# Attention into experts: zeroes at item eight, the first unit rounded at item seventeen, GpSimd's squares in halves, VectorE's order in the tail

## The chip, the core and the metric

The kernel runs on one core of a Trainium2 chip. The metric is the time of one execution on the device, in microseconds. Five engines take part: TensorE (PE, with its weight load PEld), VectorE (DVE), ScalarE (ACT), GpSimd (POOL) and SyncE (SP), which issues most of the DMAs. Each engine runs its own instructions in the order in which they stand, and waits on semaphores for the others.

## What is computed

An attention with random features, then eight experts with one expert per token, then a feed-forward layer with softplus. The inputs are float32: q, k and v of 4 x 8 x 576 x 64, 128 features; 2304 tokens of 512; experts of 512 x 1024 x 512; a last layer of 512 x 2048 x 512.

```python
def phi(x):                                   # x is q or k, scaled
    proj = np.einsum('bhsd,md->bhsm', x, omega)
    h = proj - np.sum(x * x, axis=-1, keepdims=True) / 2.0
    h = h - np.max(h, axis=-1, keepdims=True)
    return np.exp(h) / np.sqrt(m)
kv  = np.einsum('bhsm,bhsd->bhmd', k_p, v);  z = np.sum(k_p, axis=2)
num = np.einsum('bhsm,bhmd->bhsd', q_p, kv)
out = num / (np.einsum('bhsm,bhm->bhs', q_p, z)[..., None] + 1e-06)
# tokens x = out as (2304, 512)
expert_idx = np.argmax(x @ w_gate, axis=1)    # gate_w: its softmax weight
out[mask]  = gate_w * (np.maximum(x[mask] @ w1[e], 0.0) @ w2[e])     # for each expert e
h = x @ w_in
y = (np.maximum(h, 0.0) + np.log1p(np.exp(-np.abs(h)))) @ w_out
```

## The kernel before, in words

**Attention.** It goes over 20 items: for each of two pairs of batches (`bp`) five of k, then five of q. Items 0 to 4 are the first pair's k, 5 to 9 its q, 10 to 14 and 15 to 19 the second pair's. Four items of five cover 2 x 128 tokens of both batches' full rows, the middle one (a mixed item, `km` or `qm`) the remaining 64 tokens of each batch. One pass of the loop, with four slots, projects item n on PE (`pj`, L510 to L514, in three products of high and low parts) and finishes item n - 1: for k the sums `kvacc` (L564, L569), for q the transposes `tq` (L617) and the products `nm` (L634). VectorE splits the transposed input (L499), takes the maximum (L529) and makes the bias `nb` of the exponential (L533) from it and from GpSimd's half sum of squares `sq`; ScalarE takes the exponential `ph` (L535). At the end of a pair's k items, `kvacc` is copied, transposed (`kvtp`, L593), multiplied with the gate's weights (`gp`, L601) and copied to `kv` (L603), which the first `nm` reads.

**Squares.** `squares` (L446) runs on GpSimd one item ahead: one multiplication (L454), six additions that halve the width each time (L457), three small operations (L463 to L465).

**Tokens.** Of each finished q item VectorE divides `nm` (L655 to L666) into a token buffer `xt` (two of them, used in turn, for items 5, 6, 7 and so on), picks the expert (L684 to L693), makes the gate's weight (L709 to L711) and ranks the tokens (L801 to L817 with PE); SP stores the buffer to `x_tok` in DRAM (L719, or L725 in two pieces for the mixed item), and GpSimd scatters the tokens' numbers (L819).

**Zeroes.** `clear_y` issues 25 transfers of zeroes on SP's queue (L300), 5 into rows of `x_tok` (three of 128 x 513 floats, two of 64 x 513) and 20 into `y_comp` (sixteen of 128 x 512, four of 128 x 256), 5.8 MB in all. They wait for a matmul of the item named (`it.started`), item twelve here.

**First units.** A weight unit is half a matrix of an expert, 128 x 2048; it is loaded as `raw` (L237, later L260), rounded by ScalarE into the high part (L247, later L266), and VectorE takes the low part (L252, later L269). Units 0, 1 and 4 are loaded during the attention, behind items 12 and 13. Unit 0 is rounded in the slots 0 and 1 of pass `NI - 5`, 15, that is while the second pair changes from k to q. Units 1 and 4 have their low parts behind the split of the first expert's tokens.

**Tail.** The last items' tokens do not go through DRAM for the first expert: `tail_h`, `tail_l` (L714, L715) hold them, PE gathers them into `xtp`, and `first_split` rounds (L791) and splits (L792) them in four parts. The tokens for others are also stored (`x_tok<-own`). `places` makes each expert's place: `key` (L1103), `more`, `rank` (L1115) and so on to `eid_i`, which SP reads for the next expert's tokens (L975); GpSimd gathers them (L979). The experts follow: `a` from `xh`, `xl` (L966 to L968), `hh` (ScalarE, L1041) and `hl` (VectorE, L1042), `y` from these. A scheduler orders each engine by readiness; `behind` adds an order between two instructions of an engine, and `latest` holds the instruction that others are to stay behind.

Of the kernel before, what the change touches and what calls it, by code (L numbers as in the profile page):

```python
# [10 lines left out]
F32 = mybir.dt.float32  # L11
# [5 lines left out]
ALU = mybir.AluOpType  # L17
# [12 lines left out]
def tile_favor_moe_softplus(  # L30
# [14 lines left out]
    nc = tc.nc  # L45
    B, H, S, D = q.shape
# [194 lines left out]
            reason="the transfer waits for its turn")  # L241
        return raw

    latest, first_raw = {}, []

    def round_raw(i, raw, last):
        ins = nc.scalar.activation(ring[i % NRING][:, 0:1024], raw, AF.Copy)  # L247
# [41 lines left out]
    with ExitStack() as actx:  # L289
# [157 lines left out]
        def squares(it):  # L447
            src = xin[it.bp, it.kind][it.r // 4][:, :, it.r % 4:it.r % 4 + it.nr, :]
            x2 = wk.tile([P, H, it.nr, D], F32, tag="x2", bufs=1, name="x2")
            if it is items[0]:  # L450
                for h in range(0, H, 4):
                    nc.scalar.activation(x2[:, h:h + 4], src[:, h:h + 4], AF.Square)
            else:
                nc.gpsimd.tensor_tensor(x2, src, src, op=ALU.mult)  # L454
                n = D // 2
                while n:
                    nc.gpsimd.tensor_tensor(x2[:, :, :, 0:n], x2[:, :, :, 0:n], x2[:, :, :, n:2 * n],  # L457
                                            op=ALU.add)
                    n //= 2
                it.sq = sm.tile([P, H, it.nr], F32, tag="sq", bufs=4, name="sq")  # L460
                up = sm.tile([P, H, it.nr], F32, tag="up", bufs=2, name="up")
                whole = x2[:, :, :, 0]
                nc.gpsimd.tensor_scalar(it.sq, whole, 0.5 * SCALE * SCALE, None, op0=ALU.mult)  # L463
                nc.gpsimd.tensor_scalar(up, it.sq, LNM, None, op0=ALU.add)
                nc.gpsimd.tensor_tensor(it.sq, up, it.sq, op=ALU.subtract)  # L465
            it.x2 = x2
# [237 lines left out]
        def route_gate(it):  # L704
# [7 lines left out]
            for i, t in enumerate(it.tiles if it in tail else ()):  # L712
                x, g = it.xg[:, i, 0:DM], it.xg[:, i, DM:DM + 1]
                nc.scalar.activation(tail_h[t], x, AF.Copy, scale=g)  # L714
                nc.vector.scalar_tensor_tensor(tail_l[t], x, g, tail_h[t].bitcast(F32),  # L715
                                               op0=ALU.mult, op1=ALU.subtract)
            if n == 2:
                t0 = (2 * it.bp + it.r // 4) * S
                nc.sync.dma_start(  # L719
# [54 lines left out]
        def first_split():  # L774
# [15 lines left out]
            for kk in range(KD):  # L790
                nc.scalar.activation(xh[:, kk, 0:n], tp[kk][:, 0:n], AF.Copy)  # L791
                latest["DVE"] = nc.vector.tensor_tensor(  # L792
                    xl[:, kk, 0:n], tp[kk][:, 0:n], xh[:, kk, 0:n].bitcast(F32), op=ALU.subtract)
            for args in first_raw:
                rest_of_raw(*args)
            return xh, xl

        def route_rank(it):
# [50 lines left out]
        def at(step, slot, fn, *a):  # L849
            late.setdefault((step, slot), []).append((fn, a))  # L850
# [12 lines left out]
        for n in range(NI + 2):  # L863
# [46 lines left out]
                loads(1)  # L910
            if n == 2:
                clear_ids(it.started)
            if n == 12:
                clear_y(it.started)
            if n == 10:
                loads_q(1)
            for i in UNITS_AT.get(n, ()):
                raw = load_raw(i, it.started)
                if i:
                    at(NI, 3, round_raw, i, raw, True)  # L920
                    first_raw.append((i, raw, True))
                else:
                    at(NI - 5, 0, round_raw, i, raw, True)
                    at(NI - 5, 1, rest_of_raw, i, raw, False)
            if n == NI - 2:

                a, b = (inp.tile([P, VO], F32, tag="kf", bufs=2, name="tail") for _ in range(2))
# [172 lines left out]
    def places():  # L1100

        key = tb.tile([P, E], F32, tag="over", name="key")
        nc.vector.scalar_tensor_tensor(key, cntb, float(E), iota_e, op0=ALU.mult,  # L1103
                                       op1=ALU.subtract)

        def rows(a):
            return a.rearrange("p (o e) -> p o e", o=1).to_broadcast([P, R, R])
# [16 lines left out]
        nc.vector.tensor_reduce(cntp[:, 1:E], more, axis=AX.X, op=ALU.add)  # L1124

        off = tb.tile([P, E + 1], F32, tag="off", name="off")
        nc.vector.memset(off[:, E:E + 1], float(NT))
        mc = tb.tile([P, E], F32, tag="nwin", name="mc")
        nc.vector.tensor_tensor(mc, cntp, caps, op=ALU.min)
        for e in reversed(range(E)):  # L1130
# [286 lines left out]
```

## Time and profile before

| what | value |
|---|---|
| median of 3 runs | 845.51 us (845.38 to 845.65) |
| profiled execution, its own time | 852.04 us |
| span of its instructions | 850.3 us |
| TensorE's granted clock, mean | 0.991 |
| PE busy | 823.5 us (97%) |
| PEld, DVE, ACT, POOL busy | 763.8, 490.9, 475.9, 222.5 us |

A row of the timeline gives the start and the duration of an instruction (or of several of a line in succession), its engine, line and tiles, and in square brackets how long the engine had been idle before it and what ended that. In a table by windows each engine has its busy time in the window; a granted clock of 1.00 is 2.4 GHz and 0.50 is 1.2 GHz.

### The profile page before, as it was taken

What the parts mean: (1) busy time and instruction counts of PE and PEld (TensorE: products, weight loads), DVE (VectorE), ACT (ScalarE), POOL (GpSimd) and SP (SyncE); (2) the same over time, 40 slices, a digit from 0 to 9 for tenths busy, and PEclk for the clock granted to TensorE, in tenths of its full rate; (3) what the DMA queues carried; (4) which work ended last, traced back from release to release, by engine and by line L of the source; (5) the groups of instructions that cost most, each with busy time, mean ns of one, the idle gap of its engine ahead of it and who ended that gap; (6) DMA issues with size and microseconds to landing.
All of it is one profiled execution on the core that took longest, in us unless ns stands there. A gap on an engine that the chain in (4) does not pass through costs nothing.

```text
span 850.3 us, 14078 instructions
## 1 busy us (share of the span) xinstructions
PE 823.5 (97%) x5127; PEld 763.8 (90%) x5129; DVE 490.9 (58%) x1056; ACT 475.9 (56%) x1053; POOL 222.5 (26%) x361
## 2 busy tenths in 40 slices
PE   8998998998999999999999999999999999999995
PEld 6897998987999999999999999999999999999994
DVE  6678976786787677777678666542232223222221
ACT  4686757763564455566555655565455446445442
POOL 6886889223111011101035333211001001001001
PEclk9999998999999999999999999999999999999998
DMA  9962277024896888889853321030001000000001
GB/s 224 225 180 68 72 156 242 26 69 109 263 292 214 267 255 245 278 253 306 277 185 101 124 79 45 1 112 38 1 5 70 1 1 38 1 0 38 1 1 39
DMA packets 83307, 104.21 MB, mean 123 GB/s; under 512 B 16904, under 2 KB 62632, under 8 KB 83234
## 3 DMA queue, kind: packets, MB, share of 16 engines
q1 hardware_dynamic: 79442, 93.35, 36.8%
q0 software_dynamic: 3792, 9.92, 3.5%
q8 instruction: 42, 0.69, 0.4%
q14 instruction: 31, 0.25, 0.1%
HBM read 78.68 MB, written 24.58 MB: 121 GB/s over the span
## 4 chain that ended last, share of the span: by engine, by line
PE 49%; issue 35%; DMA 7%; DVE 3%; POOL 3%; ACT 2%; SPq 1%; POOLq 0%; ACTq 0%; DVEq 0%
PE a L966 6%; PE a L968 6%; PE a L967 6%; PE y L967 4%; PE y L968 4%; PE y L966 4%; PE nm L634 4%; DMA raw<-in_moe_w_dram 2%; PE kvacc L564 2%; PE o L1253 2%; PE o L1251 2%; PE o L1248 2%; POOL out_dram L1268 2%; DMA y_comp<-w 2%; PE tq L617 2%
## 5 line engine op out<-in xcount | busy, mean ns | idle before, releaser
L1236 DVE SCALAR_TENSOR_TENSOR ab<-a,ab 128x384 f32<-128x384 f32 x96 | 53.4, 556 | 161.8 <-ACT ab L1235 151.1
L966 PE MATMUL a<-yh,w 128*128 128x384 f32 x384 | 129.6, 337 | 0.0
L968 PE MATMUL a<-yh,w 128*128 128x384 f32 x384 | 129.5, 337 | 0.0
L967 PE MATMUL a<-yl,w 128*128 128x384 f32 x384 | 129.0, 336 | 0.0
L1253 PE MATMUL o<-w,gl 128*128 128x512 f32 x288 | 114.0, 397 | 0.0
L1251 PE MATMUL o<-w,gh 128*128 128x512 f32 x288 | 113.9, 396 | 0.0
L1248 PE MATMUL o<-w,gh 128*128 128x512 f32 x288 | 112.9, 393 | 0.1
L1233 ACT ACTIVATE ab<-a 128x384 f32<-128x384 f32 x96 | 47.1, 491 | 113.0 <-PE a L968 112.9
L269 DVE TENSOR_TENSOR w<-raw,w 128x1024 fp32r<-128x1024 f32 x69 | 84.2, 1222 | 26.6 <-ACT w L266 25.9
L535 ACT ACTIVATE ph<-pj,nb 128x128 f32<-128x128 f32 x288 | 82.2, 395 | 30.0 <-DVE nb L533 21.0
L266 ACT ACTIVATE w<-raw 128x1024 fp32r<-128x1024 f32 x69 | 72.8, 1057 | 37.6 <-DMA raw<-in_moe_w_dram 37.3
L1268 POOL DMA_INDIRECT out_dram<-ob,idx x18 | 17.6, 976 | 280.7 <-ACT ob L1266 277.2
L1240 DVE TENSOR_TENSOR gl<-ab,gh 128x384 fp32r<-128x384 f32 x96 | 60.6, 631 | 52.1 <-ACT gh L1239 52.1
L1239 ACT ACTIVATE gh<-ab 128x384 fp32r<-128x384 f32 x96 | 50.4, 525 | 54.0 <-DVE ab L1236 53.7
L967 PE MATMUL y<-hl,w 128*128 128x344 f32 (+6 forms) x256 | 78.7, 308 | 0.0
L968 PE MATMUL y<-hh,w 128*128 128x344 f32 (+6 forms) x256 | 78.1, 306 | 0.0
L966 PE MATMUL y<-hh,w 128*128 128x344 f32 (+6 forms) x256 | 75.8, 306 | 1.4 <-ACT hh L1041 1.4
L967 PEld LDWEIGHTS a<-yl,w 128*128 128x128 f32 x384 | 72.4, 189 | 4.2
L966 PEld LDWEIGHTS a<-yh,w 128*128 128x128 f32 x384 | 72.2, 188 | 4.4 <-DVE ab L1236 0.2
L968 PEld LDWEIGHTS a<-yh,w 128*128 128x128 f32 x384 | 72.0, 188 | 0.0
L966 PE MATMUL a<-xh,w 128*128 128x344 f32 (+6 forms) x224 | 69.1, 309 | 0.3 <-DVE hl L1042 0.3
L968 PE MATMUL a<-xh,w 128*128 128x344 f32 (+6 forms) x224 | 67.7, 302 | 0.0
(231 smaller groups left out, 1879.6 us busy)
## 6 DMA issues: line engine op xcount, KB each, us to landing
raw<-in_moe_w_dram SPq DMA_DIRECT2D x64, 512.0 KB
raw<-in_moe_w_in_dram SPq DMA_DIRECT2D x16, 512.0 KB
raw<-in_moe_w_out_dram SPq DMA_DIRECT2D x16, 512.0 KB
yb<-y_comp SPq DMA_DIRECT2D x6, 768.0 KB
vf<-in_v_dram SPq DMA_DIRECT2D x4, 1024.0 KB
qf<-in_q_dram SPq DMA_DIRECT2D x4, 1024.0 KB
y_comp<-w SPq DMA_DIRECT2D x16, 256.0 KB
wi_f<-cvr SPq DMA_DIRECT2D x16, 256.0 KB
```

The lines of the kernel that those rows point to most:

```text
L266: ins = nc.scalar.activation(slot[:, c:c + 1024], raw[:, c:c + 1024], AF.Copy)
L269: nc.vector.tensor_tensor(slot[:, 1024 + c:1024 + c + 1024], raw[:, c:c + 1024], slot[:, c:c + 1024].bitcast(F32), op=ALU.subtract)
L535: ins = nc.scalar.activation(dst[j], pj[:, j // 2, j % 2, :], AF.Exp, bias=nb[:, j // 2, j % 2:j % 2 + 1])
L966: nc.tensor.matmul(o, lhsT=wH, rhs=xH, start=first, stop=False)
L967: nc.tensor.matmul(o, lhsT=wH, rhs=xL, start=False, stop=False)
L968: nc.tensor.matmul(o, lhsT=wL, rhs=xH, start=False, stop=last)
L1236: nc.vector.scalar_tensor_tensor(ab, a, 0.0, ab, op0=ALU.max, op1=ALU.add)
L1239: placed[0] = nc.scalar.activation(gh, ab, AF.Copy)
L1240: placed[1] = nc.vector.tensor_tensor(gl, ab, gh.bitcast(F32), op=ALU.subtract)
L1248: ins = nc.tensor.matmul(os[t], lhsT=gh[:, s], rhs=u[:, c:c + DM], start=f == 0, stop=False)
L1251: nc.tensor.matmul(os[t], lhsT=gh[:, s], rhs=u[:, 1024 + c:1024 + c + DM], start=False, stop=False)
L1253: ins = nc.tensor.matmul(os[t], lhsT=gl[:, s], rhs=u[:, c:c + DM], start=False, stop=f == NF2 - 1)
```

## The change

- `clear_y` is called at item eight, not twelve.
- Unit 0's two steps of rounding are asked for at pass `NI - 3`, 17.
- Units 1 and 4 have their low parts asked for at pass `NI + 1`, slot 3, no longer behind the split of the first expert's tokens.
- GpSimd's multiplication, and the first of the six additions, run in two halves of four heads each.
- `tail_l` becomes the instruction that VectorE's later ones stay behind; `key` and the first write of `off` stay behind the split of the tokens.

```diff
--- before.py
+++ after.py
@@ -241,7 +241,7 @@
             reason="the transfer waits for its turn")
         return raw
 
-    latest, first_raw = {}, []
+    latest = {}
 
     def round_raw(i, raw, last):
         ins = nc.scalar.activation(ring[i % NRING][:, 0:1024], raw, AF.Copy)
@@ -451,11 +451,17 @@
                 for h in range(0, H, 4):
                     nc.scalar.activation(x2[:, h:h + 4], src[:, h:h + 4], AF.Square)
             else:
-                nc.gpsimd.tensor_tensor(x2, src, src, op=ALU.mult)
+
+                for h in range(0, H, 4):
+                    hs = slice(h, h + 4)
+                    nc.gpsimd.tensor_tensor(x2[:, hs], src[:, hs], src[:, hs], op=ALU.mult)
                 n = D // 2
                 while n:
-                    nc.gpsimd.tensor_tensor(x2[:, :, :, 0:n], x2[:, :, :, 0:n], x2[:, :, :, n:2 * n],
-                                            op=ALU.add)
+                    step = 4 if n > D // 4 else H
+                    for h in range(0, H, step):
+                        a = x2[:, h:min(h + step, H)]
+                        nc.gpsimd.tensor_tensor(a[:, :, :, 0:n], a[:, :, :, 0:n],
+                                                a[:, :, :, n:2 * n], op=ALU.add)
                     n //= 2
                 it.sq = sm.tile([P, H, it.nr], F32, tag="sq", bufs=4, name="sq")
                 up = sm.tile([P, H, it.nr], F32, tag="up", bufs=2, name="up")
@@ -712,8 +718,8 @@
             for i, t in enumerate(it.tiles if it in tail else ()):
                 x, g = it.xg[:, i, 0:DM], it.xg[:, i, DM:DM + 1]
                 nc.scalar.activation(tail_h[t], x, AF.Copy, scale=g)
-                nc.vector.scalar_tensor_tensor(tail_l[t], x, g, tail_h[t].bitcast(F32),
-                                               op0=ALU.mult, op1=ALU.subtract)
+                latest["DVE"] = nc.vector.scalar_tensor_tensor(
+                    tail_l[t], x, g, tail_h[t].bitcast(F32), op0=ALU.mult, op1=ALU.subtract)
             if n == 2:
                 t0 = (2 * it.bp + it.r // 4) * S
                 nc.sync.dma_start(
@@ -791,8 +797,6 @@
                 nc.scalar.activation(xh[:, kk, 0:n], tp[kk][:, 0:n], AF.Copy)
                 latest["DVE"] = nc.vector.tensor_tensor(
                     xl[:, kk, 0:n], tp[kk][:, 0:n], xh[:, kk, 0:n].bitcast(F32), op=ALU.subtract)
-            for args in first_raw:
-                rest_of_raw(*args)
             return xh, xl
 
         def route_rank(it):
@@ -910,7 +914,7 @@
                 loads(1)
             if n == 2:
                 clear_ids(it.started)
-            if n == 12:
+            if n == 8:
                 clear_y(it.started)
             if n == 10:
                 loads_q(1)
@@ -918,10 +922,10 @@
                 raw = load_raw(i, it.started)
                 if i:
                     at(NI, 3, round_raw, i, raw, True)
-                    first_raw.append((i, raw, True))
+                    at(NI + 1, 3, rest_of_raw, i, raw, True)
                 else:
-                    at(NI - 5, 0, round_raw, i, raw, True)
-                    at(NI - 5, 1, rest_of_raw, i, raw, False)
+                    at(NI - 3, 0, round_raw, i, raw, True)
+                    at(NI - 3, 1, rest_of_raw, i, raw, False)
             if n == NI - 2:
 
                 a, b = (inp.tile([P, VO], F32, tag="kf", bufs=2, name="tail") for _ in range(2))
@@ -1100,8 +1104,9 @@
     def places():
 
         key = tb.tile([P, E], F32, tag="over", name="key")
-        nc.vector.scalar_tensor_tensor(key, cntb, float(E), iota_e, op0=ALU.mult,
-                                       op1=ALU.subtract)
+        ins = nc.vector.scalar_tensor_tensor(key, cntb, float(E), iota_e, op0=ALU.mult,
+                                             op1=ALU.subtract)
+        behind(ins, latest["DVE"])
 
         def rows(a):
             return a.rearrange("p (o e) -> p o e", o=1).to_broadcast([P, R, R])
@@ -1124,7 +1129,7 @@
         nc.vector.tensor_reduce(cntp[:, 1:E], more, axis=AX.X, op=ALU.add)
 
         off = tb.tile([P, E + 1], F32, tag="off", name="off")
-        nc.vector.memset(off[:, E:E + 1], float(NT))
+        behind(nc.vector.memset(off[:, E:E + 1], float(NT)), ins)
         mc = tb.tile([P, E], F32, tag="nwin", name="mc")
         nc.vector.tensor_tensor(mc, cntp, caps, op=ALU.min)
         for e in reversed(range(E)):
```

On SP's queue, from the store of item five's tokens to the loads of the first units, before (`xt_944`, `xt_1115`, `xt_1272`, `xt_1459`, `xt_1646` are the buffers of items 5 to 9, `qf_1718` the last load of q, `w11_80` the zeroes):

```order
L719 DMA x_tok_67<-xt_944 128x1026
L719 DMA x_tok_67<-xt_1115 128x1026
L368 DMA qf_1718<-in_q_dram 128x8x256
L725 DMA x_tok_67<-xt_1272 64x513 x2
L719 DMA x_tok_67<-xt_1459 128x1026
L719 DMA x_tok_67<-xt_1646 128x1026
L300 DMA x_tok_67<-w11_80 128x513 x3
L300 DMA x_tok_67<-w11_80 64x513 x2
L300 DMA y_comp_70<-w11_80 128x512 x4
...
L237 DMA raw_1970<-in_moe_w1_dram 128x4x256
```

and of the changed kernel (items 5 to 9 are `xt_958`, `xt_1131`, `xt_1290`, `xt_1504`, `xt_1693`, the last load of q `qf_1765`):

```order
L725 DMA x_tok_67<-xt_958 128x1026
L300 DMA x_tok_67<-w11_80 128x513 x2
L725 DMA x_tok_67<-xt_1131 128x1026
L300 DMA x_tok_67<-w11_80 128x513
L300 DMA x_tok_67<-w11_80 64x513 x2
L300 DMA y_comp_70<-w11_80 128x512 x4
...
L731 DMA x_tok_67<-xt_1290 64x513 x2
L368 DMA qf_1765<-in_q_dram 128x8x256
L725 DMA x_tok_67<-xt_1504 128x1026
L725 DMA x_tok_67<-xt_1693 128x1026
L237 DMA raw_1996<-in_moe_w1_dram 128x4x256
```

The zeroes moved from behind the tokens of item 9 to between those of item 6 and item 7; the last load of q and three stores of tokens stand behind them.

On VectorE, the first write of item 9's token buffer, which waits for the DMAs that store item 7's from the same buffer; before:

```order
L655 SCALAR_TENSOR_TENSOR rc_1650<-eps_1648,nm_1639 128x6 [waits PE_49]
L658 RECIPROCAL rc_1650<-rc_1650 128x6 [waits DVE_49]
L662 TENSOR_TENSOR lgp_1647<-nm_1639,rc_1650 128x3x16 [waits DVE_49]
L666 TENSOR_TENSOR xt_1646<-nm_1639,rc_1650 128x3x2x64 [waits DMAHW3_49,DMAHW2_49]
L709 TENSOR_REDUCE xt_1459<-ex_1599 128x2 [waits Activation_49]
```

and in the changed kernel:

```order
L668 TENSOR_TENSOR lgp_1694<-nm_1686,rc_1697 128x3x16 [waits DVE_49]
L715 TENSOR_REDUCE xt_1504<-ex_1646 128x2 [waits Activation_49]
...
L821 CAST si_1682<-sl_1680 128x2 [waits DMASW3_49,DMASW2_49,DVE_49]
L538 TENSOR_REDUCE mx_1753<-pj_1717 128x4 [waits PE_49]
L672 TENSOR_TENSOR xt_1693<-nm_1686,rc_1697 128x3x2x64 [waits DMAHW3_49,DMAHW2_49]
L539 TENSOR_TENSOR nb_1752<-sq_1454,mx_1753 128x4 [waits DVE_49]
```

The write stands eleven operations further behind its `lgp`, and a `nb` of the item then projected stands right behind it. Lines of the changed kernel are 4 to 7 higher there (L672 is L666, L539 is L533).

On VectorE in the tail, before:

```order
L715 SCALAR_TENSOR_TENSOR tail<-own,tail 128x512
L949 COPY cntb<-ct 128x8
L1123 COPY cntp<-cntb 128x1
L792 TENSOR_TENSOR w_81<-xtp_3127,w_80 128x344
L1103 SCALAR_TENSOR_TENSOR key<-cntb,iota_e 128x8
L1127 MEMSET off 128x1
L792 TENSOR_TENSOR w_81<-xtp_3128,w_80 128x344
L1113 TENSOR_TENSOR more<-key 128x49
L792 TENSOR_TENSOR w_81<-xtp_3129,w_80 128x344
L792 TENSOR_TENSOR w_81<-xtp_3130,w_80 128x344
L252 TENSOR_TENSOR w_73<-raw,w_73 128x1024
L252 TENSOR_TENSOR w_76<-raw,w_76 128x1024
```

and in the changed kernel:

```order
L721 SCALAR_TENSOR_TENSOR tail<-own,tail 128x512
L252 TENSOR_TENSOR w_73<-raw,w_73 128x1024
L252 TENSOR_TENSOR w_76<-raw,w_76 128x1024
L953 COPY cntb<-ct 128x8
L1128 COPY cntp<-cntb 128x1
L798 TENSOR_TENSOR w_81<-xtp_3165,w_80 128x344
L798 TENSOR_TENSOR w_81<-xtp_3166,w_80 128x344
L798 TENSOR_TENSOR w_81<-xtp_3167,w_80 128x344
L798 TENSOR_TENSOR w_81<-xtp_3168,w_80 128x344
L1107 SCALAR_TENSOR_TENSOR key<-cntb,iota_e 128x8
L1132 MEMSET off 128x1
```

The two low parts of units 1 and 4 stand ahead of the four splits (`w_81<-xtp`), and `key` behind them.

## Rows read from the trace of the kernel before

**Rows 1.** The table by windows of 50 us: the window, then the busy time of PE, PEld, DVE, ACT and POOL (and their instructions), the granted clock, the DMA engines' busy share, GB/s.

```profile
100.00:150.00 50.00, 46.27 (x363) 44.40 (x363) 36.74 (x80) 31.47 (x101) 44.11 (x79) 0.92 0.63 180
...
250.00:300.00 50.00, 50.00 (x328) 49.00 (x327) 36.34 (x57) 24.00 (x39) 4.45 (x5) 1.00 0.78 250
```

**Rows 2.** The timeline from 137 to 146 us, where the second pair changes from k to q.

```profile
138.05 0.66 PE L617 MATMUL tq<-ident,ph 128*128 128x128 f32 x4 [0.54 <-DVE w L499]
...
139.02 1.06 ACT L247 ACTIVATE w<-raw 128x1024 fp32r<-128x1024 f32 x1 [0.72 <-DMA raw<-in_moe_w_dram]
...
139.57 1.89 POOL L454 TENSOR_TENSOR x<-qf 128x1024 f32<-128x1024 f32 x1
...
140.11 2.44 DVE L252 TENSOR_TENSOR w<-raw,w 128x1024 fp32r<-128x1024 f32 x1 [1.05 <-ACT w L247]
...
141.44 0.55 PE L593 MATMUL kvtp<-ident,kv 128*128 128x128 f32 x3 [1.43 <-ACT ph L535]
...
143.36 2.07 PE L634 MATMUL nm<-kv,qT 128*128 128x128 f32 x8 [0.61 <-DVE kv L603]
```

**Rows 3.** The timeline at 75 to 84 us and at 112 to 119 us: VectorE's operations beside GpSimd's, and PE's waits behind them.

```profile
75.06 1.89 POOL L454 TENSOR_TENSOR x<-kf 128x1024 f32<-128x1024 f32 x1
75.26 1.72 DVE L686 TENSOR_TENSOR dl<-lg,rmx 128x16 f32<-128x16 f32 x1
...
77.02 0.17 DVE L688 SCALAR_TENSOR_TENSOR cand<-dl,desc 128x16 f32<-128x16 f32 x1
...
78.49 0.17 PE L801 MATMUL rk<-oh,tri_b 128*128 128x16 bf16 x1 [1.71 <-DVE oh L693]
...
83.54 0.63 PE L617 MATMUL tq<-ident,ph 128*128 128x128 f32 x4 [1.05 <-DVE rc L658]
...
115.72 1.87 DVE L533 TENSOR_TENSOR nb<-sq,mx 128x4 f32<-128x4 f32 x1
116.29 3.63 POOL L457 TENSOR_TENSOR x<-x 128x512 f32<-128x512 f32 x6
...
118.10 1.01 PE L569 MATMUL kvacc<-vm,ph 128*128 128x130 f32 x6 [1.07 <-ACT ph L535]
```

**Rows 4.** The table by windows of 5 us, with the columns of rows 1.

```profile
80.00:85.00 5.00, 3.52 (x33) 2.96 (x32) 4.81 (x20) 3.12 (x10) 1.90 (x6) 1.00 0.60 176
...
100.00:105.00 5.00, 4.95 (x45) 4.91 (x45) 5.00 (x14) 2.48 (x7) 4.09 (x8) 1.00 0.26 105
...
120.00:125.00 5.00, 5.00 (x46) 5.00 (x45) 4.23 (x8) 4.00 (x14) 4.76 (x7) 1.00 1.02 136
125.00:130.00 5.00, 5.00 (x43) 4.71 (x41) 4.19 (x5) 2.75 (x11) 4.59 (x9) 1.00 1.06 374
...
140.00:145.00 5.00, 2.95 (x15) 2.39 (x15) 4.35 (x7) 4.08 (x14) 4.84 (x5) 0.73 0.32 104
145.00:150.00 5.00, 5.00 (x26) 5.00 (x25) 1.39 (x4) 1.74 (x5) 4.36 (x12) 0.50 0.10 33
150.00:155.00 5.00, 5.00 (x36) 5.00 (x35) 3.16 (x10) 1.78 (x6) 0.43 (x3) 0.75 0.00 0
155.00:160.00 5.00, 5.00 (x46) 5.00 (x45) 4.28 (x13) 4.59 (x15) 0.00 (x0) 1.00 0.00 0
```

**Rows 5.** The timeline of SP's issues, and of VectorE where it writes item 9's token buffer (the second number of an SP row runs from the first issue to the end of the last).

```profile
80.55 0.34 SPq L719 DMA_DIRECT2D x_tok<-xt  x1
...
90.66 1.15 SPq L725 DMA_DIRECT2D x_tok<-xt  x2
...
98.49 0.55 DVE L666 TENSOR_TENSOR xt<-nm,rc 128x384 f32<-128x384 f32 x1
...
114.03 2.46 SPq L300 DMA_DIRECT2D x_tok<-w  x5
116.53 16.25 SPq L300 DMA_DIRECT2D y_comp<-w  x20
132.93 1.79 SPq L237 DMA_DIRECT2D raw<-in_moe_w_dram  x3
```

**Rows 6.** The timeline of the tail, 199 to 208 us: VectorE's splits, `key`, units 1 and 4, and who waits.

```profile
200.01 0.52 DVE L792 TENSOR_TENSOR w<-xtp,w 128x344 fp32r<-128x344 f32 x1 [3.42 <-ACT w L791]
...
202.10 0.17 DVE L1103 SCALAR_TENSOR_TENSOR key<-cntb,iota_e 128x8 f32<-128x8 f32 x1 [1.57 <-DMA x_tok<-own]
...
202.76 0.42 PE L967 MATMUL a<-w,w 128*128 128x344 f32 x1 [0.96 <-DVE w L792]
203.59 2.35 DVE L252 TENSOR_TENSOR w<-raw,w 128x1024 fp32r<-128x1024 f32 x2
...
206.43 0.46 ACT L1041 ACTIVATE hh<-a 128x344 fp32r<-128x344 f32 x1 [5.40 <-DVE rank L1115]
...
206.94 0.89 PE L966 MATMUL y<-hh,w 128*128 128x344 f32 x4 [1.39 <-ACT hh L1041]
```

**Rows 7.** The groups by line and form: GpSimd's operations by size, their number, busy time, and mean ns of one.

```profile
L457 POOL TENSOR_TENSOR x<-x 128x512 f32<-128x512 f32 x15 | 19.1, 1276 | 0.1
...
L454 POOL TENSOR_TENSOR x<-qf 128x1024 f32<-128x1024 f32 x8 | 15.1, 1894 | 0.0
...
L457 POOL TENSOR_TENSOR x<-x 128x256 f32<-128x256 f32 x19 | 13.9, 730 | 0.9
...
L454 POOL TENSOR_TENSOR x<-qm 128x512 f32<-128x512 f32 x2 | 2.1, 1040 | 0.0
```

## The prediction

> **What bounds the kernel now.** I read a table by windows of 50 us first [rows 1]. TensorE is the engine that is full: from 250 us on it does not stand still, 50.00 of 50 us in the window that begins there, while in 100:150 it lacks 3.73 us and the granted clock is 0.92. Nothing that this change touches after that point can shorten the run, so only the attention stage and its tail into the experts count, the first 215 us or so. There PE's waits name their releasers [rows 2, 3, 6]: VectorE or ScalarE in the middle of the attention, then VectorE's splits and ScalarE's `hh` in the tail. GpSimd appears in no wait of PE, but it shows up inside VectorE's durations. The profiled execution took 852.04 us, 6.53 more than the median of 845.51; I take it that a difference counted in the trace carries over to the median one to one.
>
> **The costliest spot lies at 139 to 155 us.** ScalarE rounds unit 0's weights (L247) at 139.02, after 0.72 us of waiting for `raw`. VectorE's remainder (L252) begins at 140.11 and takes 2.44 us, with GpSimd's 1.89 us square beside it [rows 2]; the two remainders of the tail together took 2.35 us [rows 6], some 1.2 each. Behind these two, PE waits 1.43 us (the exponentials queue behind L247 on ScalarE) and 0.61 us (the kv copy L603 queues behind L252 on VectorE). Right behind, the granted clock is 0.73, 0.50 and 0.75 in three windows of 5 us [rows 4]. That is the lower of the two levels (1.2 in place of 2.4 GHz), and costs 0.27 x 5 + 0.50 x 5 + 0.25 x 5 = 5.1 us of work at the full clock, a stretch of some 10.2 us.
>
> **Unit 0 two items later (term 1, 2).** The rounding leaves the hand-over of k to q: 1.43 + 0.61 = 2.0 us of PE idle go, and I count the 5.1 us of clock as gone with them, because the window behind, 155:160, is at 1.00 with PE full [rows 4]. The 0.54 us just ahead [rows 2] waits for another operation, L499 behind ScalarE's `xT`, and I let half a microsecond of such small waits go, since PE arrives later after what follows below. At its new place, item 17, GpSimd does nothing (busy 0.00 of 5 us in 155:160) while PE is 5.00 of 5 full [rows 4], so I cost L247 and L252 at 0 there; if that cover fails, the delay is one L252 and one L247, 2.3 us.
>
> **The zeroes at item eight (term 5, 6).** Before, 25 zero transfers begin to issue at 114.03 and end at 132.78, 18.75 us, and PE's row does not suffer: DMA share is 1.06 in 125:130 with PE at 5.00 [rows 4, 5]. Moving them takes nothing from PE by itself; it frees `raw`, which was issued only at 132.93 and reached ScalarE at 139.0, 6.1 us later. What matters is what now stands behind the zeroes on SP's queue: the two stores of `xt_1290`, item seven's tokens. In the old order this store is issued at 90.66 and the buffer is written again by L666 at 98.49, with no wait [rows 5]. In the new order the bulk of the zeroes goes out behind the store that was ready at 80.55, so the store of `xt_1290` issues at about 80.55 + 18.75 less some 0.9 for the two zeroes that go ahead = 98.4. By the row of `raw` it lands up to 6.1 us later, 104.5; it is 128 KB and not 512 KB, which at the 374 GB/s of 125:130 is 1 us less, so 103.4. VectorE wants the buffer for `xt_1693` (L672, item nine's first product) at the old 98.49, plus some 2 us because eleven small operations now stand ahead, less the port gains below: about 100. VectorE is then held 3 to 4.5 us. Queued behind L672 on VectorE is L539 (`nb`), ScalarE's exponentials wait for that and PE's `kvacc` sums for these. How much cushion PE has is told by the tokens' row at 75 to 78: L686 was 1.55 us longer than its short form, and PE stood 1.71 us [rows 3], so hardly any; with VectorE at 5.00 of 5 in 100:105 [rows 4] there is no spare time before it either. I take 3.0 us of PE idle, with bounds of 0 (the transfers land early) and 9.5 (below).
>
> Does the clock fall there? At 80:85 PE was busy 3.52 of 5 us, with waits in pieces of 1.05 us and less (1.71 us at 78), at clock 1.00; at 140:143.4 it stood 1.43 and 0.61 us close together, hardly ran between, and the clock fell [rows 2 to 4]. One piece of 3 us is nearer to the second. I take a second stretch like the one removed, **+5.1 us**, with bounds 0 and 10.2 (two). So the forecast has the low-clock stretch moved from 142 to about 103, not removed.
>
> **GpSimd in halves (term 3).** Before, L686 at 75.26 takes 1.72 us (0.17 for the sibling L688 next to it) and ends with GpSimd's L454 of 75.06 + 1.89; `nb` at 115.72 takes 1.87 and ends with an L457 [rows 3]. So VectorE is held until a GpSimd instruction ends. PE's waits that hang on this are 1.71, 1.05 and 1.07 us [rows 3]. Halving leaves at worst 1.04 of 1.89 and 0.73 of 1.28 [rows 7]: 0.85 + 0.55 + 0.55 = 2.0 us. The price is 2 x 1.04 - 1.89 + 2 x 0.73 - 1.28 = 0.37 us of GpSimd for each full item, some 5.5 us in all fifteen; PE waits for GpSimd nowhere, but GpSimd is busy 44.11 of 50 us in 100:150 [rows 1], so if `sq` comes late up to 1 us is lost. I take -2.0, bounds -3.5 (the same in the first 60 us) and +1.
>
> The Trainium skill (SBUF — State Buffer, section "SBUF: two separate sides") calls the pair of ports that VectorE shares with GpSimd an exclusive lock, held for the whole instruction, and not a split of bandwidth. By that the halves give the 2.0 us; were it a split, the same bytes would cost the same time and the term would be 0 or above. The ends of L686 and L454, 76.98 and 76.95, agree with the lock.
>
> **VectorE's order in the tail (term 4).** Before, the split L792 is done at 200.53, and the key (L1103) waits 1.57 us for the DMA `x_tok<-own`; the other splits are behind it, so PE waits 0.96 us. Then 2.35 us of L252 stand ahead of `rank`, ScalarE's `hh` waits for `rank` and PE's first `y` waits 1.39 us [rows 6]. After, the four splits run in a row, the two L252 lie in VectorE's 3.42 us of idle ahead of them, and the key comes behind: 0.96 + 1.39 = 2.35 less about 0.25 for the small operations that now run ahead of `hl`: -2.1. If the DMA of `own` is later still, this drops to 0.
>
> **Sum.** -2.0 - 5.1 - 0.5 - 2.0 - 2.1 + 3.0 + 5.1 = -3.6: 852.04 - 3.6 = 848.4 profiled, and 845.51 - 3.6 = **841.9 us**.
>
> **Rivals.**
> (a) The store of `xt_1290` lands before VectorE needs it, or the idle is broken in pieces as at 80:85, and the clock stays at 1.00. For it: the zeroes are 5.8 MB, and at the 374 GB/s of 125:130 [rows 4] these need 15.4 us, not 18.75. Against: 18.75 us is what their issuing took with no other transfer of SP's among them. Time: -11.7 + 3.0 = -8.7, 836.8; with 0 of stall 833.8.
> (b) The stall eats the gain: 6 us of idle and 5.1 of clock against 11.7. 844.9, no difference. For it: VectorE carries a backlog out of such a stall, and has little room to work it off (100:105 at 5.00 of 5).
> (c) Slower: the zeroes go at the 136 GB/s of 120:125 for part of their way, the store lands at about 110, and PE stands 9.5 us with one stretch of low clock: 14.6 - 11.7 = +2.9, 848.4. It decides from a stall of 6.6 us on (no gain) and is over 0.2% slower from 8.3 us on. For it: rows 4's 120:125; against: that window did not hold the whole issuing back, which is in the 18.75 us.
> (d) The rounding holds nothing up but only hides another wait at the hand-over, so terms 1 and 2 do not come and the stall adds its own: -4.6 + 3.0 + 5.1 = +3.5, 849.0. Against: both releasers there are the rounding's own queues.
>
> **Chances.** Forecast 0.42, (a) 0.25, (b) 0.16, (c) 0.10, (d) 0.07. Some 1.7 us (0.2%) is what a measurement of this kernel can tell from no change. Faster holds (a) and most of the forecast, whose own range is 840 to 844: 0.62. Same: (b) and the edge of the forecast: 0.21. Slower: 0.17. The range leaves out (c), (d) and the best part of (a): 835.0 to 846.5.
>
> **What would show it.** The L672 that writes `xt_1693` with a wait for DMA of 3 to 4.5 us at about 100 to 104; PE idle there before `kvacc`, and windows below 1.00 just behind. At 138 to 155 windows at 1.00 and no 2.44 us L252. L686, L533 and L710 (now some lines lower) at most about 1 us long beside GpSimd. In the tail four splits in a row, no wait of PE on them, and `hh` at once. The prediction is wrong if the clock never falls after 20 us (then (a)), if GpSimd turns up as a releaser of VectorE's `nb` for more than 2 us in all, or if PE stands over 6 us near 103.

## The result, and the profile after

| kernel | median | runs | ratio to the kernel before, 95% interval |
|---|---|---|---|
| before | 845.44 us (844.53 to 845.65) | 4 | 1 |
| changed | 857.14 us (853.59 to 857.51) | 4 | 1.0131 [1.0103, 1.0159] |

The change makes the kernel 1.3% slower, 11.7 us by the medians and 11.1 by the ratio. The forecast was 841.9 us and the range ended at 846.5.

The profiled execution of the changed kernel took 857.46 us, with a span of 855.7 us. PE's waits, in all, number and longest, are first to read there; they answer to the brackets of [rows 2, 3, 6].

```profile
PE kvacc L561 <- DVE xt L672: 9.6, 1, 9.6
PE y L970 <- ACT hh L1045: 2.9, 1, 2.9
...
PE rk L805 <- DVE oh L699: 2.2, 2, 1.6
...
PE xtp L1001 <- ACT xg L994: 1.7, 1, 1.7
```

One wait is larger than all others: 9.6 us before the sums of item eleven's k, for VectorE's `xt`. The timeline of the changed kernel, SP from 79 to 104 us and then VectorE, PE and ScalarE at 113 us, shows it as the prediction had drawn it, only larger (it answers to [rows 5]).

```profile
79.63 0.82 SPq L300 DMA_DIRECT2D x_tok<-w  x2
80.72 0.32 SPq L725 DMA_DIRECT2D x_tok<-xt  x1
81.09 2.63 SPq L300 DMA_DIRECT2D x_tok<-w  x3
83.77 18.59 SPq L300 DMA_DIRECT2D y_comp<-w  x20
102.89 1.10 SPq L731 DMA_DIRECT2D x_tok<-xt  x2
...
112.98 0.56 DVE L672 TENSOR_TENSOR xt<-nm,rc 128x384 f32<-128x384 f32 x1 [11.40 <-DMA x_tok<-xt]
...
113.59 0.59 PE L561 MATMUL kvacc<-zero_b 128*128 128x512 bf16 x1 [9.60 <-DVE xt L672]
113.64 2.28 ACT L541 ACTIVATE ph<-pj,nb 128x128 f32<-128x128 f32 x8 [11.04 <-DVE nb L539]
```

Item seven's store is issued at 102.89, behind the zeroes; VectorE has been idle for 11.40 us when it may write `xt_1693` at 112.98. The table by windows of the changed kernel (columns as in rows 1, answering to [rows 4]) has the clock behind this.

```profile
105.00:110.00 5.00, 0.00 (x0) 0.00 (x0) 0.00 (x0) 0.00 (x0) 3.67 (x8) 0.76 0.95 96
110.00:115.00 5.00, 1.41 (x6) 1.32 (x6) 2.02 (x6) 1.36 (x5) 0.00 (x0) 0.50 0.75 245
115.00:120.00 5.00, 5.00 (x33) 4.81 (x31) 4.26 (x19) 2.89 (x11) 0.39 (x2) 0.71 0.02 7
...
140.00:145.00 5.00, 5.00 (x47) 5.00 (x46) 2.75 (x8) 4.42 (x17) 4.83 (x8) 1.00 0.00 0
...
210.00:215.00 5.00, 4.97 (x22) 4.98 (x23) 4.96 (x12) 3.77 (x6) 0.78 (x1) 0.66 0.78 232
```

The low clock at 142 us is gone; one like it stands at 105 to 120 us, of 0.24 x 5 + 0.50 x 5 + 0.29 x 5 = 5.2 us. PE stood through more than half of it, so what it cost is less: 0.50 x 1.41 + 0.29 x 5.00 = 2.2 us, from PE's busy time in its last two windows. A short one is new at 210 us, 0.34 x 5 = 1.7 us. It follows on the second wait, in the tail; there the timeline of the changed kernel answers to [rows 6].

```profile
198.99 2.35 DVE L252 TENSOR_TENSOR w<-raw,w 128x1024 fp32r<-128x1024 f32 x2
...
199.58 1.47 POOL L823 DMA_INDIRECT id_slot<-tok,si  x1 [0.30 <-issue]
...
201.36 0.97 POOL L823 DMA_INDIRECT id_slot<-tok,si  x1 [0.31 <-DVE w L252]
...
202.77 1.78 DVE L798 TENSOR_TENSOR w<-xtp,w 128x344 fp32r<-128x344 f32 x4 [1.16 <-ACT w L797]
204.72 0.17 DVE L1107 SCALAR_TENSOR_TENSOR key<-cntb,iota_e 128x8 f32<-128x8 f32 x1 [0.16 <-issue]
...
209.51 0.46 ACT L1045 ACTIVATE hh<-a 128x344 fp32r<-128x344 f32 x1 [5.72 <-DMA id_slot<-tok,si]
...
210.03 1.51 PE L970 MATMUL y<-hh,w 128*128 128x344 f32 x4 [2.94 <-ACT hh L1045]
```

The four splits run in a row and `key` waits no more, as forecast. But the first `hh` waits for the landing of GpSimd's last scatter of `id_slot`, where [rows 6] put its wait down to `rank`; E8 below shows which of the two it had been before.

### The profile page after: what moved, and what is told of

The parts are those of the page before. It is cut to its first block, busy times and chain, and to the rows that moved or that the text cites. A ratio compares the mean times of both kernels' runs of the same rounds, so it can differ in the third digit from the quotient of the medians.

```text
span 855.7 us, 14115 instructions
## 1 busy us (share of the span) xinstructions
PE 819.7 (96%) x5128; PEld 762.3 (89%) x5129; DVE 483.4 (56%) x1056; ACT 476.6 (56%) x1053; POOL 230.0 (27%) x399
## 4 chain that ended last, share of the span: by engine, by line
PE 51%; issue 34%; DMA 7%; DVE 3%; POOL 2%; ACT 1%; SPq 0%; POOLq 0%; DVEq 0%
PE a L970 6%; PE a L972 6%; PE a L971 6%; PE y L971 4%; PE y L972 4%; PE y L970 4%; PE kvacc L570 4%; PE nm L640 3%; PE o L1258 2%; PE o L1256 2%; PE o L1253 2%; POOL out_dram L1273 2%; DMA y_comp<-w 2%; PE pj L516 2%; PE pj L520 1%
## 5 line engine op out<-in xcount | busy, mean ns | idle before, releaser
L269 DVE TENSOR_TENSOR w<-raw,w 128x1024 fp32r<-128x1024 f32 x69 | 84.2, 1221 | 22.7 <-ACT w L266 22.2
L970 PE MATMUL a<-xh,w 128*128 128x344 f32 (+6 forms) x224 | 69.1, 308 | 0.0
L1045 ACT ACTIVATE hh<-a 128x344 fp32r<-128x344 f32 (+6 forms) x64 | 27.3, 427 | 74.1 <-PE a L972 68.3
```

Of the source, the lines that this page charges most:

```text
L269: nc.vector.tensor_tensor(slot[:, 1024 + c:1024 + c + 1024], raw[:, c:c + 1024], slot[:, c:c + 1024].bitcast(F32), op=ALU.subtract)
L970: nc.tensor.matmul(o, lhsT=wH, rhs=xH, start=first, stop=False)
```

## The experiments

All ratios are to the kernel before, run on the same chip as the experiment.

**E1, the changed kernel with the zeroes back at item twelve.**

```diff
-            if n == 8:
+            if n == 12:
                 clear_y(it.started)
```

> The changed kernel with the zeroes back at item twelve, the rest as changed. Theory (the zeroes hold the store of item seven's tokens, and VectorE's write of item nine's waits for that store): PE's single wait of 9.60 us and the stretch of low clock behind it (5.1 us) go, 857.1 - 14.7 = 842.4 us. Rival (the loss of 11.7 us is in the tail, in the halves and in unit 0's new place): at most the stall of 9.6 us is won and a low clock turns up at another place, 850 us or more.

843.08 us, 0.9976 [0.9966, 0.9986], close to the theory's 842.4. So moving the zeroes costs 14.1 us here by the medians (13.1 by the ratios), and all the rest of the change together gains some 2. Its windows at the two places (columns as in rows 1):

```profile
105.00:110.00 5.00, 5.00 (x45) 4.90 (x45) 3.06 (x10) 2.19 (x8) 4.83 (x11) 1.00 0.26 105
...
140.00:145.00 5.00, 5.00 (x47) 5.00 (x46) 3.96 (x15) 3.59 (x11) 4.59 (x11) 1.00 0.02 6
```

**E2, the changed kernel with the zeroes at item nine.** The store of item seven's tokens then stands behind three zeroes and not behind 25.

```diff
-            if n == 8:
+            if n == 9:
                 clear_y(it.started)
```

> The changed kernel with the zeroes at item nine: the store of item seven's tokens is now ahead of all but three of them, while the zeroes still run beside the same stage, 89 to 113 us. Theory (a wait for a buffer, nothing else): no wait of VectorE over 1 us for a store, no low clock, 842 us as with item twelve. Rival (the zeroes' traffic itself slows the stage, whatever stands behind them): above 850 us, with waits of PE at 95 to 115 us.

842.03 us, 0.9968 [0.9955, 0.9982]. The store and the zeroes on SP, and the first write of item nine's buffer on VectorE:

```profile
87.89 1.29 SPq L300 DMA_DIRECT2D x_tok<-w  x3
89.28 1.15 SPq L731 DMA_DIRECT2D x_tok<-xt  x2
90.47 1.24 SPq L300 DMA_DIRECT2D x_tok<-w  x2
91.75 17.54 SPq L300 DMA_DIRECT2D y_comp<-w  x20
...
97.17 0.55 DVE L672 TENSOR_TENSOR xt<-nm,rc 128x384 f32<-128x384 f32 x1
```

The zeroes run at 88 to 109 us, across the place where the changed kernel stood, and VectorE waits for no store there. It is the order on SP, not the traffic: the rival is out. The trace does have low clock, 0.90 and 0.76 in 75:80 and 80:85, but ahead of the zeroes; E7 and E10 have a stretch like it there.

**E3, the kernel before with the tail's part alone** (`key` and `off` behind the splits, units 1 and 4 rounded ahead of them).

```diff
-                    first_raw.append((i, raw, True))
+                    at(NI + 1, 3, rest_of_raw, i, raw, True)
...
+        behind(ins, latest["DVE"])
```

> The kernel before with the tail's part of the change alone (key and off behind the splits, units 1 and 4 rounded ahead of them). Theory from the trace after: the two L252 lie across GpSimd's last scatters of id_slot, the first hh waits for these scatters, PE waits 2.9 us for hh and 1.7 us for the gathered tokens, so +1 to +3 us: 846.5 to 848.5. Rival (the tail's part is worth 2.1 us, as the prediction had it, and its loss in the trace after comes from the zeroes): 843.3 us.

846.82 us, 1.0021 [1.0011, 1.0030], 1.8 us slower. The forecast's gain of 2.1 us is not there without the zeroes either. Its timeline:

```profile
191.19 1.05 POOL L817 DMA_INDIRECT id_slot<-tok,si  x1 [0.17 <-DVE run L701]
...
192.69 2.35 DVE L252 TENSOR_TENSOR w<-raw,w 128x1024 fp32r<-128x1024 f32 x2
...
193.91 1.97 POOL L817 DMA_INDIRECT id_slot<-tok,si  x1 [0.30 <-DVE w L252]
...
202.39 0.46 ACT L1039 ACTIVATE hh<-a 128x344 fp32r<-128x344 f32 x1 [4.91 <-DMA id_slot<-tok,si]
```

GpSimd's third scatter, beside the second L252, takes 1.97 us where the first took 1.05, and the first `hh` waits for its landing: by the trace's landings it is down at 201.98, 8.1 us after its issue. PE stands 2.1 us for this `hh`, and behind that the granted clock is 0.79 and 0.87 in 200:205 and 205:210, another 0.21 x 5 + 0.13 x 5 = 1.7 us.

**E4, the kernel before with GpSimd's squares in halves alone.**

```diff
-                nc.gpsimd.tensor_tensor(x2, src, src, op=ALU.mult)
+                for h in range(0, H, 4):
+                    hs = slice(h, h + 4)
+                    nc.gpsimd.tensor_tensor(x2[:, hs], src[:, hs], src[:, hs], op=ALU.mult)
...
+                    step = 4 if n > D // 4 else H
...
```

> The kernel before with GpSimd's squares in halves alone. Theory (VectorE is held until the end of a GpSimd instruction, so halves hold it half as long): -1 to -2 us, 843.5 to 844.5; VectorE's longest small operations at 75 to 130 us about 1 us instead of 1.9. Rival (0.37 us more of GpSimd's time for each full item comes late): 846 us or more, with waits for sq.

846.40 us, 1.0025 [1.0011, 1.0039]: slower, but not for the rival's reason, since VectorE's one wait for `sq` is 0.5 us (0.6 in the first trace of the kernel before). The loss stands at the hand-over of k to q:

```profile
136.11 1.06 ACT L247 ACTIVATE w<-raw 128x1024 fp32r<-128x1024 f32 x1 [3.51 <-DMA raw<-in_moe_w_dram]
...
138.25 1.46 PE L606 MATMUL gp<-wgb,kvT 128*128 128x16 f32 x6 [2.82 <-ACT ph L540]
```

The stage reaches unit 0's rounding earlier, while `raw` still comes behind the zeroes: ScalarE stands 3.51 us (0.72 before [rows 2]) and PE 2.82. The clock falls there, too: 0.80 and 0.52 in 135:140 and 140:145, 0.20 x 5 + 0.48 x 5 = 3.4 us.

**E5, the kernel before with the zeroes at item eight alone.**

```diff
-            if n == 12:
+            if n == 8:
                 clear_y(it.started)
```

> The kernel before with the zeroes at item eight alone. Theory (the store of item seven's tokens behind the zeroes is the loss): VectorE held 9 to 11 us at about 102 to 113, the low clock behind it, 845.1 + 14 = 859 us; with the waits at the hand-over of k to q gone, since raw is there early, 856 to 860. Rival (the stall in the changed kernel needs the other edits' order too): within 3 us of the kernel before.

852.04 us, 1.0073 [1.0057, 1.0089]: slower as the theory says, but by 6.2 us and not 14, between the ranges of theory and rival. VectorE's wait in its timeline is about half as long:

```profile
107.87 0.56 DVE L666 TENSOR_TENSOR xt<-nm,rc 128x384 f32<-128x384 f32 x1 [5.97 <-DMA x_tok<-xt]
...
108.48 0.58 PE L555 MATMUL kvacc<-zero_b 128*128 128x512 bf16 x1 [4.84 <-DVE xt L666]
```

**E6, the kernel before with unit 0 at item seventeen alone.**

```diff
-                    at(NI - 5, 0, round_raw, i, raw, True)
-                    at(NI - 5, 1, rest_of_raw, i, raw, False)
+                    at(NI - 3, 0, round_raw, i, raw, True)
+                    at(NI - 3, 1, rest_of_raw, i, raw, False)
```

> The kernel before with unit 0's rounding at item seventeen alone. Theory (the hand-over's waits of 1.43 and 0.61 us hang on the rounding; the long low clock behind them was of the one profiled execution and not of the median): -2 to -3 us, 842 to 843. Rival (the clock's 5.1 us are in the median, too): 838 us. Second rival (the waits are another's): 845 us.

844.51 us, 0.9989 [0.9979, 0.9998]: 0.9 us, where the prediction had 2.0 + 5.1. It lies between the theory's 842 to 843 and the second rival's 845; the first rival's 838 is out.

**E7, the kernel before with `key` and `off` behind the splits alone** (and `tail_l` as in the changed kernel), units 1 and 4 left behind the splits.

```diff
+        behind(ins, latest["DVE"])
...
+        behind(nc.vector.memset(off[:, E:E + 1], float(NT)), ins)
```

> The kernel before with key and off behind the splits alone, units 1 and 4 left behind the splits. Theory (the loss of the tail's part comes from the two L252 across GpSimd's scatters, and the key's place alone is good): the wait of 0.96 us before the second product goes, 844.1 to 845. Rival (the key's place is the loss): 846.5 us or more.

846.81 us, 1.0017 [1.0008, 1.0026]. The rival's time, and a miss for the theory: `key`, now behind both splits and L252, costs about as much as E3's edit. But it does so in another way. The wait of 0.96 us is gone, as the theory says, the last scatter lands 4.5 us after its issue, and PE waits 0.4 us for `hh`; later in the tail PE's waits for `xg`, `hl` and `w` come to 0.9 + 0.8 + 0.3 us, where E8 has 0.8 in all. That is 1.2 us more against the 0.96 won, so most of the loss is not located; a stretch of low clock in the trace, 0.66 in 80:85, is not the tail's.

**E8, the kernel before once more, for its profile.**

> The kernel before once more, for its profile. Theory (the stretch of 10.2 us of low clock at 142 us stood in the first profiled execution and is not the rule): the wait before kvtp is under 1 us, no low clock or a short one there, and a span some 5 to 7 us below 850.3. Rival: the same stretch again.

846.86 us, with a span of 845.1. The same place as [rows 2, 4], timeline and window:

```profile
140.12 1.13 ACT L247 ACTIVATE w<-raw 128x1024 fp32r<-128x1024 f32 x1
141.29 1.23 DVE L252 TENSOR_TENSOR w<-raw,w 128x1024 fp32r<-128x1024 f32 x1 [0.23 <-ACT w L247]
142.59 1.89 POOL L454 TENSOR_TENSOR x<-qf 128x1024 f32<-128x1024 f32 x1
142.61 0.55 PE L593 MATMUL kvtp<-ident,kv 128*128 128x128 f32 x3 [0.61 <-ACT ph L535]
```

```profile
140.00:145.00 5.00, 4.33 (x36) 4.06 (x37) 4.20 (x9) 5.00 (x16) 4.67 (x8) 1.00 0.50 161
145.00:150.00 5.00, 5.00 (x47) 5.00 (x46) 3.58 (x12) 2.96 (x10) 4.44 (x10) 1.00 0.09 32
```

L252 is over before GpSimd's square begins and takes 1.23 us, PE waits 0.61 us in place of 1.43, and the clock stays at 1.00. The 2.44 us and the low clock of [rows 2, 4] were those of one execution: E3 and E7, which have the same attention stage, show 0.6 us before `kvtp` and a clock of 1.00 there, too.

In the tail, the same trace answers to the `hh` of [rows 6]:

```profile
201.68 0.46 ACT L1041 ACTIVATE hh<-a 128x344 fp32r<-128x344 f32 x1 [4.37 <-PE a L968]
202.13 0.20 DVE L1115 TENSOR_REDUCE rank<-more 128x7 f32<-128x49 f32 x1
```

Here `hh` begins ahead of `rank`, so it does not wait for it. In the first trace of the kernel before, by the trace's landings, the last scatter of `id_slot` landed at 206.02, `rank` ended at 206.05 and `hh` began at 206.43: the scatter is what it had waited for. In E8 that scatter had landed at 198.45.

**E9 and E10, zeroes at item nine and unit 0 at item seventeen on the kernel before, with halves (E9) and with whole squares (E10);** the tail is that of the kernel before in both.

```diff
-            if n == 12:
+            if n == 9:
                 clear_y(it.started)
...
-                    at(NI - 5, 0, round_raw, i, raw, True)
+                    at(NI - 3, 0, round_raw, i, raw, True)
...
```

> Zeroes at item nine, unit 0 at item seventeen and halves, with the tail as in the kernel before. Theory (the tail's part costs some 1.5 us): 840.5, below the 842.0 of the same kernel with the tail's part. Rival (in this surrounding the tail's part is neutral): 842.

> Zeroes at item nine and unit 0 at item seventeen alone, whole squares, the tail as before. Theory (halves are of no use once the hand-over is free of unit 0: waits of VectorE saved, GpSimd's time lost): 843 to 844, no better than with halves. Rival (halves cost 1.3 us here as they did alone): 839 to 840.

E9: 841.48 us, 0.9954 [0.9937, 0.9971]. E10: 845.39 us, 0.9995 [0.9980, 1.0010]. Halves are worth 3.9 us here by the medians (3.5 by the ratios), more than E10's theory or rival allowed. E9's own question stays open: 841.48 us lies between its theory and its rival, and its interval overlaps that of E2, which has the tail's part. VectorE's `nb` in 60 to 180 us, first of E9 and then of E10 (number, busy time, mean ns):

```profile
L539 DVE TENSOR_TENSOR nb<-sq,mx 128x4 f32<-128x4 f32 x18 | 4.9, 272 | 0.4
```

```profile
L533 DVE TENSOR_TENSOR nb<-sq,mx 128x4 f32<-128x4 f32 x18 | 11.0, 611 | 0.6
```

Where the 3.9 us are won is shown in part. From the first `kvtp` to the tail's first `xtp` the gaps in PE's row add up to 6.2 us in E10 and 5.3 in E9, and E10's trace has low clock, 0.97 and 0.69 in 75:80 and 80:85, which is 1.7 us. The rest is not located.

**E11, the changed kernel with whole squares, and E12, the changed kernel once more, for its profile.**

```diff
-                for h in range(0, H, 4):
-                    hs = slice(h, h + 4)
-                    nc.gpsimd.tensor_tensor(x2[:, hs], src[:, hs], src[:, hs], op=ALU.mult)
+                nc.gpsimd.tensor_tensor(x2, src, src, op=ALU.mult)
...
```

> The changed kernel with whole squares. Theory (the longer stall, 9.6 us against 4.8 us with the zeroes alone, comes with the halves, which put the store later and slow its landing): PE's wait for xt about 5 us, 850 to 853. Rival (the longer stall is another edit's, or differs from run to run): 855 to 858 with a stall near 9 us.

> The changed kernel once more, for its profile. Theory (the stall belongs to the order): PE's wait for xt 8 to 10 us and a time of 855 to 858. Rival (it differs from run to run): 4 to 7 us, 850 to 854.

E11: 852.28 us, 1.0068 [1.0044, 1.0092], PE's wait for `xt` 4.2 us. E12: 853.13 us in one run, and its timeline:

```profile
101.80 1.09 SPq L731 DMA_DIRECT2D x_tok<-xt  x2
...
108.35 0.56 DVE L672 TENSOR_TENSOR xt<-nm,rc 128x384 f32<-128x384 f32 x1 [6.57 <-DMA x_tok<-xt]
```

The same kernel holds VectorE 11.40 us in one execution and 6.57 in another, so the longer stall can't be laid on the halves by E11: its expectation was met, but E12's rival was met, too. Both are single traces. The times do not settle it either: E11's six runs took 850.80 to 853.25 us and the changed kernel's four of the result 853.59 to 857.51, but E12, run beside E11, took 853.13.

**E13, the changed kernel with item seven's two stores issued by ScalarE.**

```diff
-                    nc.sync.dma_start(x_tok[t0 + 512:t0 + S, :], it.xg[g * 64:(g + 1) * 64, 0, :])
+                    eng = nc.scalar if it.bp == 0 else nc.sync
+                    eng.dma_start(x_tok[t0 + 512:t0 + S, :], it.xg[g * 64:(g + 1) * 64, 0, :])
```

> The changed kernel, zeroes at item eight, but item seven's two stores are issued by ScalarE and not by SP. Theory (what holds VectorE is the store's place behind the zeroes on SP's queue, issue at 102 to 103): the store issues at 92 to 97 and VectorE's wait falls under 2 us, 843 to 847 with the tail's part still in. Rival (the backlog of the DMA engines holds it wherever it is issued): it lands at 105 or later, VectorE waits 4 us or more, 850 to 857.

853.23 us, 1.0099 [1.0083, 1.0115]. The time is the rival's, the mechanism neither's:

```profile
96.83 2.56 ACTq L732 DMA_DIRECT2D x_tok<-xt  x2
99.49 0.60 ACT L625 ACTIVATE qT<-tq 128x512 f32<-128x512 f32 x1 [10.20 <-DMA y_comp<-w]
...
100.14 2.08 PE L640 MATMUL nm<-kv,qT 128*128 128x128 f32 x8 [8.24 <-ACT qT L625]
...
103.22 0.42 DVE L672 TENSOR_TENSOR xt<-nm,rc 128x256 f32<-128x256 f32 x1
```

VectorE no longer waits for the store, but ScalarE stands 10.20 us, most of it for zeroes to land before it may issue, and PE stands behind it. The trace shows why: the store's first piece has the semaphore of a zero that SP issued at 89.03 and goes out at 96.83, when that zero has landed (96.75); the second has that of the zero issued at 91.97 and goes out at 98.94. On SP it is the same: in the trace after, the store's first piece has the semaphore of the zero issued at 96.73, which landed at 102.43, and goes out at 102.89. So the zeroes ahead of a store hold it from either of the two engines.

**E14, zeroes at item fourteen, behind the loads of units 0, 1 and 4;** otherwise as E9.

```diff
-            if n == 12:
+            if n == 14:
                 clear_y(it.started)
```

> Zeroes at item fourteen, behind the loads of units 0, 1 and 4 and with no store of tokens near; unit 0 at item seventeen, halves, the tail as in the kernel before. Theory (only what stands behind the zeroes matters): as with item nine, 841 to 842. Rival (the zeroes' traffic beside the load of the last q and the tokens costs something at item nine): 839 to 840.

840.91 us, 0.9960 [0.9944, 0.9977]. With E9 the lowest of all, and below both kernels; the two can't be told apart, as the theory says, and E2's interval overlaps theirs.

## Why the prediction was wrong

**The carry-over to the median failed first.** The prediction took "that a difference counted in the trace carries over to the median one to one", and set 7.1 us of gain (2.0 of idle, 5.1 of clock) on [rows 2, 4]. Its own number spoke against that: the profiled execution was 6.53 us above the median, and 5.1 us of low clock is most of it. E8 shows the place without the collision and without the low clock, and E6 gives 0.9 us for the whole edit. Together terms 1 and 2 were 6.2 us too high.

**The stall was the right mechanism, and its size was off.** The store of item seven behind the zeroes, VectorE held at item nine's first write, `nb`, the exponentials and PE behind it, a stretch of low clock: all are in the trace after, and E1 and E2 show that the place on SP is the cause. The term was +3.0 us of idle, bounds 0 and 9.5; it measured 9.60 in one trace of the changed kernel, 4.75 in the other (PE's wait behind E12's 6.57 us). Three pieces were off. The store was issued at 102.89 and 101.80, not 98.4: the zeroes took from 79.63 to 102.36, 22.7 us, and not 18.75, since each waits for an earlier one to land, and the DMA engines moved less here, 236 GB/s in 80:100 against 274 in 115:135 before. From its issue to VectorE's release it took 10.1 and 6.6 us, not 5.0. VectorE arrived at 101.6 to 101.8, not at 100, which gave back some of it. The clock's 5.1 us were foreseen for this place, and a stretch of that length came, but since PE stood through more than half of it, it cost 2.2 us.

**The tail gave a loss in place of 2.1 us.** The step that failed was "0.96 + 1.39 = 2.35": it read from [rows 6] that `hh` waits for `rank`. That releaser was only the last of several by the profile; `hh` had waited for the landing of the last scatter of `id_slot` (E8), and so an earlier `rank` could win nothing. The two L252, put where VectorE was idle, lie across these scatters on GpSimd. In all seven traces with this part of the change the last scatter lands 6.7 to 8.5 us after its issue, in eight of the nine without it 4.1 to 4.8 (7.9 in the first trace of the kernel before). Counted as free, they cost; the cover that the prediction did name was VectorE's idle time only. Not separated from this is that SP's next loads of `raw` also go out earlier with it (193.97 in E3, 198.26 in E8). E7 loses as much by `key`'s place alone, 1.4 us; why is not shown.

**The halves: the forecast of 2.0 us lies between two runs of opposite sign.** Alone they lose 2.1 us by the ratio, 1.3 by the medians (E4), as the earlier stage meets `raw` behind the zeroes; with unit 0 away from there they gain 3.9 us (E9 against E10). As an estimate, E4's 2.82 us of wait and 3.4 of low clock at the hand-over, less the 0.61 of E8 and the 3.9, make a loss of 1.7. VectorE's `nb` falls from 611 to 272 ns, as an instruction held to the end of a shorter one would. The Trainium skill's exclusive lock (SBUF — State Buffer, "SBUF: two separate sides") agrees with that. But the mechanism gave only one of the three waits that the 2.0 us were counted from: the 1.07 us before `kvacc` is gone in E9, in place of the 1.05 before `tq` stands one of 1.44 (for `w`), and the 1.71 before `rk` at 78 us [rows 3] stayed at 1.65 in the trace after. `dl` there takes 0.17 us and not 1.72, but `oh`, three operations on, now meets the halves:

```profile
76.11 2.46 DVE L699 TENSOR_TENSOR oh<-cand,cm 128x16 bf16<-128x16 f32 x1
76.51 2.03 POOL L457 TENSOR_TENSOR x<-kf 128x512 f32<-128x512 f32 x2
```

It ends at 78.57, with the second half (78.54). Two halves in a row, 2.03 us, held VectorE to the end of both, as the whole square of 1.89 us had held it to its end; E1, E4 and E9 show the same 2.45 us.

**The sum.** E1 has everything but the zeroes' new place and gains 2.0 us; the prediction had 11.7 for that. The parts agree with E1: 0.4 (E10) + 3.9 (halves) - 1.8 (E3) = 2.5. The zeroes then cost 14.1 us, where it had 8.1. So 9.7 us of the miss lie in the gains and 6.0 in the zeroes. Of the 14.1 the first trace shows 9.60 of stall, 2.2 of clock and 2.6 in the tail, where PE's waits for `hh` and `xg` are 2.9 and 1.7 us against 1.8 and 0.2 in E1; why the tail waits longer with the zeroes early is not shown. Rival (c) was nearest in its idle time of 9.5 us, and with a gain of 2.0 in place of 11.7 it would have come to 845.4 - 2.0 + 14.6 = 858.0 us, against 857.1. That is luck in part: its 5.1 us of clock were 2.2, and the tail made up the rest.

**Open.** What makes the store land in 6.6 us in one execution and 10.1 in another: in the slow one the DMA engines were 0.95 busy and moved 96 GB/s in 105:110, in E12 0.85 and 212 GB/s. The Trainium skill says that DMAs of all issuing engines run on the same 16 DMA engines and interleave (DMA: Bandwidth & Descriptors, "Issuing engines are not separate DMA queues"). No run here tests that: in E13 a semaphore held the store before its issue, which says nothing of how packets share the engines.

## What to carry to other kernels

When a bulk of transfers moves ahead on a queue, look for the first store that now stands behind it and for the tile that is written again only after that store; with two buffers in turn, the next writer but one pays. Move the bulk past the last store whose tile is soon written again: at item nine or fourteen it cost nothing that these runs can tell. When an instruction is said to wait for several, check in a second trace whether it ever starts ahead of the one named. And where the profiled execution is well above the median, ask which of its stretches the median does not have before any gain is taken from it.

## What the runs showed that was not expected

A small slip in time decides whether a two-input operation of VectorE meets a long one of GpSimd: L252 took 2.44 us in one execution of the kernel before and 1.23 in another, and a stretch of low clock stood behind it in the first alone. The low-clock stretches had different lengths, by the windows of the traces: 5.1 us lost at 142 us in the first trace of the kernel before, 1.7 us lost at 210 us in the trace after, none there in E8. GpSimd's scatters, too, take longer beside VectorE's L252, 1.97 us against 1.05 (E3): that one ends 0.8 us after L252 does (195.88 and 195.04). Halving a GpSimd operation does not halve what VectorE waits for when one half follows the other (2.46 us at `oh`). And one edit, the squares in halves, was worth -1.3 us alone and +3.9 us with two others, by the medians.
